# A fused attention and two-MLP kernel on one core: keys pooled by matmuls, a joined softmax, shared weight tiles and another order of stages

## The chip, the cores and the metric

The kernel runs on one core of a Trainium2 chip. The metric is the device time of one execution in microseconds (us); less is better. Three runs of the kernel before took 1649.82, 1650.77 and 1654.72 us; their median is 1650.77 us.

## The reference

Three layers follow one another (B = H = 8, S = 576, D = 64; 4608 tokens, model width 512, inner width 2048):

```python
k_p = k.reshape(B, H, 72, 8, D).mean(axis=3)      # keys and values pooled by 8
v_p = v.reshape(B, H, 72, 8, D).mean(axis=3)
scores = q @ k_p.T / sqrt(D)
attn = exp(scores - max(scores)); attn = attn / (sum(attn) + 1e-9)
x = (attn @ v_p) as tokens x 512                  # layer 0
h = x @ w_in_a                                    # layer 1: a rational function between two matmuls
x = ((a0 + a1 h + a2 h^2 + a3 h^3) / (1 + |b0||h| + |b1|h^2 + 1e-6)) @ w_out_a
out = relu(x @ w_in_b)^2 @ w_out_b                # layer 2
```

## The kernel before

**Tiling.** The tokens are cut into 36 chunks of 128 (for attention) and 9 blocks of 512 (for the two MLPs). Every fp32 matrix is split into a high and a low fp32r part, and a product is three matmul passes (high·high, high·low, low·high). One *slot* is one of 16 column groups of the inner width for one block: `mm1` (12 matmuls of 128x128 by 128x512), the function between (`first` and `second`, on VectorE and ScalarE), and three slots later (LAG = 3) `mm2` (12 matmuls). In the rational layer `first` and `second` put seven operations of 128x512 on VectorE and five on ScalarE; in layer 2 VectorE has one.

**Stages.** Blocks 0 and 1 come first, in 64 slots ("half"), while the weights are read and split (`w_raw`, `w_decode`) and written back to DRAM in split form. After that `w_fetch` reads a split weight tile (1 MB) for each slot. `SEQ` lists the stages after slot 63: `one` j is the rational layer of block j (16 slots), `two` 2 is layer 2 of block 2, and `pair` does layer 2 of two blocks at once by a seven-product scheme (28 slots of four steps with 6 matmuls each), with sums of the weights made beforehand (`w_sums`, `SUM_AT`) and seven combined inputs (`pair_forms`, tiles by `FORM_TAGS`). So the slots are: half 0 to 63, one 2 64 to 79, one 3 80 to 95, two 2 96 to 111, one 4 112 to 127, a gap of 3, pair (3,4) 131 to 158, one 5, one 6, gap, pair (5,6) 194 to 221, one 7, one 8, gap, pair (7,8).

**Attention.** `place_chunk` spreads each chunk over slots by `CHUNK_AT`: `q_split` at slot t, `qk`, `row_max` and `exps` at t + 2, `norm` at t + 4, `a_turn` or `a_split` at t + 5, `av` at t + 6, `x_out` at t + 7. The first nine chunks (c < NF) use fp32 matmuls on keys and values that are pooled on the core (`kv_first`): for the keys, `k_sum` reduces each of four 128x576 tiles on VectorE and scales it on ScalarE; for the values, `v_sum` pools by matmuls against a constant 0/1 matrix `sums`. The other 27 chunks use three-term bf16 products on keys and values that are pooled by adding DMAs of GpSimd's queue (`k_add`, `v_add`) and split by `k_split` and `v_split`. In `exps`, a half of a chunk in `WHOLE` takes one subtraction on VectorE, one exp on ScalarE and one sum on VectorE; any other half takes four exps on ScalarE, each with its own accumulated sum. `TURN_DVE` says which halves of the transposed weights VectorE copies out of PSUM; ScalarE copies the others. For blocks 0 to 2 (j < PLAIN) `x_out` writes the block's input straight into the tiles that `mm1` reads; for later blocks it writes to DRAM (`xd`), and `x_fetch` reads it back two slots ahead of the block.

**Order.** Nothing above is issued as it stands. `Plan` collects every operation with an assumed cost, runs a list scheduler with due times worked out backward, tries 96 variants and writes out one fixed order for each queue (TensorE, VectorE, ScalarE, GpSimd, SyncE). Each engine then works through its list in order. `run` adds lower limits: an attention operation placed at slot s (s at least 16, WINDOW = 8) isn't issued before the `mm1` (or pair step) of slot s - 8 has been; `w_sums` and `x_fetch` have no such limit. All instructions are recorded by one helper, so the profile gives nearly all of them the same line (L409), and they are told apart by their tiles: `h` and `y` are the PSUM banks of `mm1` and `mm2`, `x` and `w` inputs and weights, `sv`, `pq` and `g` the rational function, `xf`, `wi`, `gf`, `wo` the pair, `q`, `mx`, `e`, `sm`, `a`, `xo` a chunk, `kr` and `vr` the raw keys and values of the early chunks, `wv` and `ws` the weight sums.

Of the kernel before, what the change touches and what calls it, by code (L numbers as in the profile page):

```python
# [11 lines left out]
F32 = mybir.dt.float32  # L12
# [26 lines left out]
AHEAD, FIRST = 5.0, range(4)  # L39
FIRST_TWO = [0, 1]  # L40
PLAIN = 3
PAIRS = [(3, 4), (5, 6), (7, 8)]
SEQ = [
    ("one", 2), ("one", 3), ("two", 2), ("one", 4), ("pair", (3, 4)), ("one", 5), ("one", 6),
    ("pair", (5, 6)), ("one", 7), ("one", 8), ("pair", (7, 8)),
]
PAIR_SLOTS, PAIR_STEPS = 28, 4
NFT = DFF // 128
X_TAGS = {0: (4, 5), 1: (6, 0), 2: (1, 2), 3: (4, 5), 4: (6, 0), 5: (4, 5), 6: (6, 0), 7: (4, 5), 8: (6, 0)}
X_IN_W = {}  # L50
W_TAGS = {("one", j): (0, 1, 6, 7, 2, 3, 4, 5) for j in range(5, 9)}
W_TAGS |= {("one", 2): range(8), ("one", 3): range(8), ("one", 4): (0, 1, 3, 5, 6, 7, 2, 4)} | {("two", 2): (2, 3, 5, 6, 7)}
X2_TAGS = {3: "ya", 4: "yb", 5: "ya", 6: "yb", 7: "ya", 8: "yb"}
FORM_TAGS = {pair: dict(p1=1, p2=2, p5=3, p3=4, p6=5, p7=6, p4=0) for pair in PAIRS}
S_PLACES = ((0, 1, 2, 3), (2, 0, 3, 1))
LN_SHIFT = 60
SCALE = 1.0 / POOL / 8
# [2 lines left out]
QC = 1.0 + 1e-6  # L60
NF = 9
NORM_DVE = {0, 2, 3, 5} | set(range(8, NCHUNK))
WHOLE = {(c, 1) for c in range(NF)} | {(15, 1)}
TURN_DVE = {(c, 0) for c in range(NF)} | {(1, 1)}
BY_DMA = {(1, 1), (1, 3), (1, 5)}
KA, KB = 128 - SP, 2 * SP - 128
KC = SP + 2 * KB
# [3 lines left out]
NK = NF * CH // S  # L71
RAW_EARLY, STORE_EARLY, FETCH_EARLY, SUM_EARLY = 80.0, 25.0, 60.0, 40.0
SHIFT_ACT = {(1, f) for f in range(FH)} | {(3, 0), (3, 4)}
SUM_AT = {n: 49 + 4 * (n - 4) for n in range(4, 8)} | {n: 98 + 2 * n for n in range(4)}
CHUNK_AT = (
    {8 + n: 38 + 3 * n for n in range(8)} | {16 + n: 92 + 3 * n for n in range(6)}
    | {22 + n: 128 + 4 * n for n in range(6)} | {28 + n: 190 + 3 * n for n in range(8)}
)


# [335 lines left out]
def fused_kernel(  # L416
# [1 line left out]
    tc: tile.TileContext,  # L418
    qf: bass.AP,
    qt: bass.AP,  # L420
    kf: bass.AP,
    vn: bass.AP,
    vm: bass.AP,
    kt: bass.AP,
# [51 lines left out]
    def tt(n, out, in0, in1, op):  # L476
        dve(n, "tensor_tensor", out=out, in0=in0, in1=in1, op=op)
# [7 lines left out]
    def load(n, out, in_, early=None):  # L485
        plan.add("sp", 0.6, [(nc.sync.dma_start, dict(out=out, in_=in_))], n / LOAD_RATE, early)
# [19 lines left out]
    def h_bank():  # L506
        h_turn.append(0)
        return ps_h.tile([128, TB], F32, "h", f"h{len(h_turn) % 2}")
# [133 lines left out]
    def kv_first():  # L642


        k, v = ([p1.tile([128, 4 * TB], F32, n, f"x{o + i}") for i in range(2)] for o, n in ((0, "kr"), (2, "vr")))
        kr = [k[g // 3][:, g % 3 * S:(g % 3 + 1) * S].rearrange("p (k r) -> p k r", r=POOL) for g in range(H // 2)]
        vr = [v[c // 4][0:min(128, S - 128 * c), c % 4 * TB:(c % 4 + 1) * TB] for c in range(5)]
        for b, t in enumerate((k, v)):
            o = 1024 if b else S
            kp_t[b] = t[1][:, o:o + H // 2 * SP].rearrange("p (g k) -> p g k", g=H // 2)  # L650
            vp_t[b] = t[1][0:SP, 1536:2048]

        def k_sum(b):
            plan.ahead = K_AHEAD if b == 0 else 0.0
            for g in range(H // 2):
                load(128 * S * 4, kr[g], kf[b, g].rearrange("p (k r) -> p k r", r=POOL))
                dve(S, "tensor_reduce", out=kp_t[b][:, g], in_=kr[g], axis=AX.X, op=ALU.add)
                act(SP, AF.Copy, out=kp_t[b][:, g], in_=kp_t[b][:, g], scale=SCALE)
            if b == 0:
                q_first(0)  # L660

        def v_sum(b):
            plan.ahead = AHEAD if b == 0 else 0.0
            ps = h_bank()[0:SP]
            for c in range(5):
                n, o = min(128, S - 128 * c), S0W - 16 * c
                load(n * TB * 4, vr[c], vn[b, :, TB * c:TB * (c + 1)] if c < 4 else vm[b])
                pe(1.0, [dict(
                    out=ps, lhsT=sums[0:n, o:o + SP], rhs=vr[c], start=(c == 0), stop=(c == 4),
                )])  # L670
            act(DM, AF.Copy, out=vp_t[b], in_=ps)
            if b == 0:
                q_first(2)
                q_first(3)

        k_sum(0)
        plan.ahead = AHEAD
        q_first(1)
        v_sum(0)
        for c, fn in ((K1C, k_sum), (V1C, v_sum)):  # L680
            at(starts[c] + 5 if c >= 0 else -S0, "t", fn, 1)
# [120 lines left out]
    def exps(c, half):  # L802
        mx, sm, e = e_t[c]
        ps = sc_t.pop((c, half))
        hs = slice(half * (H // 2), (half + 1) * (H // 2))
        if (c, half) in WHOLE:
            n = H // 2 * SP
            tt(n, e[:, hs], ps, mx[:, hs].unsqueeze(2).to_broadcast([128, H // 2, SP]), ALU.subtract)
            act(n, AF.Exp, out=e[:, hs], in_=e[:, hs])
            dve(n, "tensor_reduce", out=sm[:, hs], in_=e[:, hs], axis=AX.X, op=ALU.add)  # L810
            return
        for hh in range(H // 2):
            h = half * (H // 2) + hh
            act(
                SP, AF.Exp, out=e[:, h, :], in_=ps[:, hh, :],
                bias=mx[:, h:h + 1], accum_out=sm[:, h:h + 1],
            )
# [83 lines left out]
    def x_out(c):  # L901
        ps = x_ps.pop(c)
        j, o = divmod(c, CPB)
        sc = 2.0 ** -A_SHIFT / POOL
        if j < PLAIN:
            if o == 0:
                xt[j] = [x_tile([128, 4, TB], "x", n) for n in X_TAGS[j]]
            x = [t[:, :, o * CH:(o + 1) * CH] for t in xt[j]]
        else:
            if o == 0:  # L910
                xd[j] = pd.tile([128, 2, 4, TB], F32, f"xd{j}")
            t = p2.tile([128, 2, 4, CH], F32R, "xo", "xs")
            x = [t[:, a] for a in (HI, LO)]
        act(TB, AF.Copy, out=x[HI], in_=ps, scale=sc)
        stt(TB, x[LO], ps, sc, f32(x[HI]), ALU.mult, ALU.subtract)
        if j >= PLAIN:
            for a in (HI, LO):
                load(2 ** 18, xd[j][:, a, :, o * CH:(o + 1) * CH], f32(x[a]))

# [40 lines left out]
    def evac(u):  # L960
# [16 lines left out]
        if ph == 1:  # L977
            for d in range(4):
                tt(TB, xt[j][LO][:, d], t[:, d], f32(xt[j][HI][:, d]), ALU.subtract)

    def evac_one(j):
        y = yps.pop(("one", j))
        if j < PLAIN:
            for d in range(4):
                act(TB, AF.Copy, out=xt[j][HI][:, d], in_=y[d])
                tt(TB, xt[j][LO][:, d], y[d], f32(xt[j][HI][:, d]), ALU.subtract)
            return
        if len(X2_TAGS[j]) == 2 and X2_TAGS[j][0] == "y":
            t = p1.tile([128, 4, TB], F32, "xm", X2_TAGS[j])
            x2[j] = [t[:, 0:2], t[:, 2:4]]  # L990
        else:
            x2[j] = [p2.tile([128, 2, TB], F32, "xm", X2_TAGS[j]) for _ in range(2)]
        for d in range(4):
            act(TB, AF.Copy, out=x2[j][d // 2][:, d % 2], in_=y[d])
# [239 lines left out]
    def run(slot, key):  # L1234
        for fn, args in todo.pop((slot, key), []):
            if args and args[0] in FIRST and fn in (k_add, v_add, q_load, qk, row_max, exps, norm, a_turn, av, x_out):
                plan.ahead = AHEAD
            if fn not in (w_raw, w_decode, w_sums, x_fetch, pair_forms) and slot >= GATED:
                plan.after = started.get(slot - WINDOW)
            if fn.__name__ in ("k_sum", "v_sum"):  # L1240
                plan.after = turned.get(K1C if fn.__name__ == "k_sum" else V1C)
            fn(*args)
            plan.ahead, plan.after = 0.0, None
# [44 lines left out]


    slots = [("half", (j, ph), f) for ph in range(4) for j in FIRST_TWO for f in range(FH)]  # L1290
    begins = {}
    for what, x in SEQ:
        if what == "pair" and slots[-1][0] == "one":
            slots += [("gap", None, None)] * LAG
        begins[what, x] = len(slots)
        slots += [(what, x, f) for f in range(PAIR_SLOTS if what == "pair" else NFT)]
    N = len(slots)
    steps = {pair: pair_steps(pair) for pair in PAIRS}
    for n, t in SUM_AT.items():
        for part in range(2):  # L1300
            at(t + 2 * part if n >= 4 else t, "x", w_sums, n, part, "w1" if n < 4 and part else "x3")
    for j in range(PLAIN, NB):
        at(begins["one", j] - 2, "x", x_fetch, j)
    FORMS_AT = {
        pair: begins["pair", pair] - 1 for pair in PAIRS
# [6 lines left out]
    def tile_slot(i):  # L1312

        what, x, f = slots[i]
        if what == "half":
            j, ph = x
            return j, ph // 2, wt_of[ph, f], x, f == 0, f == FH - 1, evac
        layer = int(what == "two")
        if i not in wf_t:
            wf_t[i] = w_fetch(x, layer, f)  # L1320
        done = evac_two if layer else evac_one
        return x, layer, wf_t[i], (what, x), f == 0, f == NFT - 1, lambda u: done(u[1])

# [79 lines left out]
```

## Time and profile before

| | |
|---|---|
| median of three runs | 1650.77 us |
| the profiled execution: time, span | 1649.59 us, 1647.9 us |
| TensorE, VectorE, ScalarE busy | 98 %, 86 %, 69 % |
| mean granted TensorE clock | 0.996 of full speed |
| moved by DMA | 401 MB, 244 GB/s over the span |

Busy shares are averages over stages with different limits. A matmul is issued before the one ahead of it has ended, so TensorE's busy time also covers short stalls; how many matmuls a stretch holds tells more.

### The profile page before, as it was taken

Reading aid. Unit: us, or ns where it says so; the run is one execution under the profiler, and the core shown is the slowest. Engines: PE = TensorE matmul, PEld = TensorE weight load, DVE = VectorE, ACT = ScalarE, POOL = GpSimd, SP = SyncE. Lnnn points to the kernel's source line nnn. Section 1 sums busy time; section 2 is a strip of 40 time slices with the busy share of each in tenths; the row PEclk is TensorE's granted clock in tenths of the full one; section 3 lists DMA queues with packets and bytes.
Section 4 is the critical chain, followed back from the end, with each engine's and each line's share of the span. In section 5 each row is a group of like instructions: output and inputs, shape, how many; then the busy total and the mean of one; then the engine's idle time right before and its main releaser. Section 6 shows DMA issues by size and latency. Waiting matters only on the chain.

```text
span 1647.9 us, 23637 instructions
## 1 busy us (share of the span) xinstructions
PE 1610.9 (98%) x8476; PEld 1307.3 (79%) x8476; DVE 1410.0 (86%) x2135; ACT 1132.6 (69%) x2105; POOL 77.8 (5%) x95
## 2 busy tenths in 40 slices
PE   7899999999999999999999999999999999999998
PEld 4678888888888877877787878887888788888886
DVE  7999998589889998488979788999889799996666
ACT  5989778787557766566787645667987466657553
POOL 0001100100001000001111000010000000000000
PEclk9999999999999999999999999999999999999999
DMA  7357578997999879999999996785799985555544
GB/s 269 131 231 196 152 265 298 241 257 250 313 299 286 289 258 274 322 270 279 258 243 281 283 321 245 233 244 190 227 267 263 292 291 200 185 185 171 191 154 141
DMA packets 199141, 401.43 MB, mean 244 GB/s; under 512 B 68752, under 2 KB 118768, under 8 KB 170864
## 3 DMA queue, kind: packets, MB, share of 16 engines
q1 hardware_dynamic: 188512, 379.76, 70.6%
q0 software_dynamic: 10512, 20.16, 7.8%
q8 instruction: 67, 1.10, 0.3%
q14 instruction: 50, 0.41, 0.1%
HBM read 310.91 MB, written 72.35 MB: 233 GB/s over the span
## 4 chain that ended last, share of the span: by engine, by line
PE 70%; DVE 19%; ACT 4%; DMA 3%; issue 2%; SPq 0%; ACTq 0%; DVEq 0%
PE h L409 30%; PE y L409 22%; DVE pq L409 7%; PE yx L409 7%; PE yz L409 5%; PE hz L409 5%; DVE g L409 3%; DVE sv L409 2%; ACT sv L409 2%; PE xp L409 1%; PE sc L409 1%; DMA xd<-xo 1%; DMA t<-a 1%; DVE t L409 1%; DVE wv L409 1%
## 5 line engine op out<-in xcount | busy, mean ns | idle before, releaser
L409 PE MATMUL h<-x,w 128*128 128x512 f32 x2304 | 557.8, 392 | 10.7 <-DVE pq L409 5.1
L409 PEld LDWEIGHTS h<-x,w 128*128 128x128 f32 x2304 | 430.8, 188 | 107.5 <-DVE pq L409 8.9
L409 PE MATMUL y<-g,w 128*128 128x512 f32 x1728 | 418.8, 391 | 3.7 <-DVE g L409 3.6
L409 PEld LDWEIGHTS y<-g,w 128*128 128x128 f32 x1728 | 324.1, 188 | 73.7 <-DVE g L409 6.3
L409 ACT ACTIVATE sv<-sv,cs 128x512 f32<-128x512 f32 x288 | 208.3, 724 | 154.7 <-DVE sv L409 149.8
L409 ACT ACTIVATE sv<-h 128x512 f32<-128x512 f32 x192 | 114.0, 594 | 68.1 <-PE h L409 52.7
L409 PE MATMUL h<-xf,wi 128*128 128x512 f32 x576 | 145.7, 391 | 0.7 <-ACT gb L409 0.5
L409 PE MATMUL yx<-gf,wo 128*128 128x512 f32 x576 | 142.8, 391 | 0.4 <-DVE acc L409 0.4
L409 PE MATMUL y<-w,g 128*128 128x512 f32 x576 | 140.4, 392 | 0.1
L409 ACT ACTIVATE pq<-h,cs 128x512 f32<-128x512 f32 x144 | 111.8, 776 | 24.4 <-PE h L409 14.0
L409 PEld LDWEIGHTS yx<-gf,wo 128*128 128x128 f32 x576 | 107.6, 188 | 24.3 <-issue 0.8
L409 PEld LDWEIGHTS h<-xf,wi 128*128 128x128 f32 x576 | 107.4, 188 | 23.8 <-ACT gb L409 1.4
L409 PEld LDWEIGHTS y<-w,g 128*128 128x128 f32 x576 | 107.2, 188 | 23.3 <-DVE g L409 0.5
L409 DVE SCALAR_TENSOR_TENSOR g<-pq,cs,sv 128x512 fp32r<-128x512 f32 x144 | 107.6, 747 | 19.5 <-ACT sv L409 16.9
L409 DVE SCALAR_TENSOR_TENSOR sv<-sv,cs 128x512 f32<-128x512 f32 x144 | 107.3, 745 | 14.4 <-ACT sv L409 14.3
L409 ACT ACTIVATE sv<-h,cs 128x512 f32<-128x512 f32 x144 | 98.8, 686 | 25.0 <-DVE g L409 15.9
L409 PE MATMUL hz<-xf,wi 128*128 128x512 f32 x432 | 110.2, 392 | 1.8 <-DVE ga L409 1.0
L409 PE MATMUL yz<-gf,wo 128*128 128x512 f32 x432 | 108.3, 392 | 3.1 <-DVE gf L409 1.5
L409 DVE SCALAR_TENSOR_TENSOR pq<-pq,cs 128x512 f32<-128x512 f32 x144 | 107.5, 747 | 1.9
L409 DVE SCALAR_TENSOR_TENSOR pq<-pq,cs,h 128x512 f32<-128x512 f32 x144 | 106.7, 741 | 0.6 <-ACT sv L409 0.2
L409 DVE TENSOR_TENSOR pq<-pq,h 128x512 f32<-128x512 f32 x144 | 98.0, 680 | 8.4 <-ACT pq L409 5.2
L409 DVE SCALAR_TENSOR_TENSOR pq<-sv,g 128x512 f32<-128x512 f32 x144 | 99.1, 688 | 2.8
(147 smaller groups left out, 2072.6 us busy)
## 6 DMA issues: line engine op xcount, KB each, us to landing
w<-ws SPq DMA_DIRECT2D x128, 1024.0 KB, 6.3
ws<-w SPq DMA_DIRECT2D x32, 1024.0 KB, 4.9
wi<-wf SPq DMA_DIRECT2D x48, 512.0 KB, 5.2
wo<-wf SPq DMA_DIRECT2D x48, 512.0 KB, 5.9
wo<-ws SPq DMA_DIRECT2D x72, 256.0 KB, 4.2
raw<-wa SPq DMA_DIRECT2D x16, 1024.0 KB, 6.7
raw<-wb SPq DMA_DIRECT2D x16, 1024.0 KB, 8.1
wf<-ws SPq DMA_DIRECT2D x16, 1024.0 KB, 9.2
```

Of the source, the lines that this page charges most:

```text
L409: made = fn(**{k: v.real() if isinstance(v, View) else v for k, v in kw.items()})
```

## The change

- `k_sum` pools the keys of the first two batches by matmuls: five loads of 128 (the last 64) rows of 512, four matmuls each against `sums`, one scaled copy out of PSUM. The host lays the keys out as it does the values.
- For the first nine chunks both halves are in `WHOLE`, and their exp and sum are joined into one operation each (`MERGED`); `TURN_DVE` is empty.
- The rational layers of the two blocks of a pair become one stage `both` (a, b) of 32 slots: the first 8 slots of a, all 16 of b, the last 8 of a. A weight tile is fetched once and used for both blocks (`kept`). The first half of a's output is copied out of PSUM (`evac_half`), and the second is added to it on VectorE.
- The pair's blocks are named in the other order, (4, 3) for (3, 4), and the tiles of the seven forms are given out anew.
- Layer 2 of block 2 moves from slots 96 to 111 to slots 112 to 127, behind the rational layers of blocks 3 and 4; its weight sums move along, with a lower limit.
- Block 3's input is written straight into its tiles (`DIRECT`).
- Chunks 8 to 15 stay. Chunks 16 to 19 move from slots 92 to 101 to slots 62, 66, 70 and 74; chunks 20 to 27 from 104 to 148 to 114 to 149, one each 5 slots; chunks 28 to 35 from 190 to 211 to 166 to 208, one each 6 slots.

```diff
-PAIRS = [(3, 4), (5, 6), (7, 8)]
+PAIRS = [(4, 3), (6, 5), (8, 7)]
 SEQ = [
-    ("one", 2), ("one", 3), ("two", 2), ("one", 4), ("pair", (3, 4)), ("one", 5), ("one", 6),
-    ("pair", (5, 6)), ("one", 7), ("one", 8), ("pair", (7, 8)),
+    ("one", 2), ("both", (3, 4)), ("two", 2), ("pair", (4, 3)), ("both", (5, 6)), ("pair", (6, 5)),
+    ("both", (7, 8)), ("pair", (8, 7)),
 ]
+DIRECT = {0, 1, 2, 3}
...
-FORM_TAGS = {pair: dict(p1=1, p2=2, p5=3, p3=4, p6=5, p7=6, p4=0) for pair in PAIRS}
+FORM_TAGS = {pair: dict(p1=1, p2=2, p5=3, p6=6, p3=0, p7=4, p4=5) for pair in PAIRS[1:]}
+FORM_TAGS[PAIRS[0]] = dict(p1=4, p2=5, p5=6, p6=0, p3=3, p7=1, p4=2)
...
-WHOLE = {(c, 1) for c in range(NF)} | {(15, 1)}
-TURN_DVE = {(c, 0) for c in range(NF)} | {(1, 1)}
+MERGED = set(range(NF))
+WHOLE = {(c, h) for c in MERGED for h in range(2)} | {(15, 1)}
+TURN_DVE = set()
...
-SUM_AT = {n: 49 + 4 * (n - 4) for n in range(4, 8)} | {n: 98 + 2 * n for n in range(4)}
+SUM_AT = {n: 49 + 4 * (n - 4) for n in range(4, 8)} | {n: 114 + 2 * n for n in range(4)}
 CHUNK_AT = (
-    {8 + n: 38 + 3 * n for n in range(8)} | {16 + n: 92 + 3 * n for n in range(6)}
-    | {22 + n: 128 + 4 * n for n in range(6)} | {28 + n: 190 + 3 * n for n in range(8)}
+    {8 + n: 38 + 3 * n for n in range(4)} | {12 + n: 50 + 3 * n for n in range(4)} | {16 + n: 62 + 4 * n for n in range(4)}
+    | {20 + n: 114 + 5 * n for n in range(8)} | {28 + n: 166 + 6 * n for n in range(8)}
 )
...
         def k_sum(b):
             plan.ahead = K_AHEAD if b == 0 else 0.0
-            for g in range(H // 2):
-                load(128 * S * 4, kr[g], kf[b, g].rearrange("p (k r) -> p k r", r=POOL))
-                dve(S, "tensor_reduce", out=kp_t[b][:, g], in_=kr[g], axis=AX.X, op=ALU.add)
-                act(SP, AF.Copy, out=kp_t[b][:, g], in_=kp_t[b][:, g], scale=SCALE)
+            ps = h_bank()[:, 0:H // 2 * SP].rearrange("p (g k) -> p g k", g=H // 2)
+            for c in range(5):
+                n = min(128, S - 128 * c)
+                load(n * TB * 4, kr[c], kn[b, :, TB * c:TB * (c + 1)] if c < 4 else km[b])
+                m = n // POOL
+                pe(0.4, [dict(
+                    out=ps[:, g, 16 * c:16 * c + m], lhsT=kr[c][:, 128 * g:128 * (g + 1)],
+                    rhs=sums[0:n, S0W:S0W + m], start=True, stop=True,
+                ) for g in range(H // 2)])
+            act(H // 2 * SP, AF.Copy, out=kp_t[b], in_=ps, scale=SCALE)
...
             tt(n, e[:, hs], ps, mx[:, hs].unsqueeze(2).to_broadcast([128, H // 2, SP]), ALU.subtract)
+            if c in MERGED:
+                if half == 0:
+                    return
+                n, hs = H * SP, slice(0, H)
             act(n, AF.Exp, out=e[:, hs], in_=e[:, hs])
             dve(n, "tensor_reduce", out=sm[:, hs], in_=e[:, hs], axis=AX.X, op=ALU.add)
...
+    def evac_half(j):
+        y = yps.pop(("half one", j))
+        t = p1.tile([128, 4, TB], F32, "xm", X2_TAGS[j])
+        ysb[j] = t
+        for d in range(4):
+            act(TB, AF.Copy, out=t[:, d], in_=y[d])
+
     def evac_one(j):
         y = yps.pop(("one", j))
+        if j in ysb:
+            t = ysb.pop(j)
+            for d in range(4):
+                tt(TB, t[:, d], y[d], t[:, d], ALU.add)
+            x2[j] = [t[:, 0:2], t[:, 2:4]]
+            return
...
+            if fn is w_sums and args[0] < 4:
+                plan.after = started.get(slot - 2)
...
+        if what == "both":
+            a, b = x
+            begins["one", a], begins["one", b] = len(slots), len(slots) + FH
+            for f in range(FH):
+                kept[len(slots) + FH + f] = len(slots) + f
+                kept[len(slots) + 3 * FH + f] = len(slots) + 2 * FH + f
+            slots += [("one", a, f) for f in range(FH)] + [("one", b, f) for f in range(NFT)]
+            slots += [("one", a, f) for f in range(FH, NFT)]
+            continue
```

## Rows read from the trace of the kernel before

**Rows 1.** The page, part 1: TensorE, busy us, share of the span, instructions

```profile
PE 1610.9 (98%) x8476; PEld 1307.3 (79%) x8476; DVE 1410.0 (86%) x2135; ACT 1132.6 (69%) x2105; POOL 77.8 (5%) x95
```

**Rows 2.** Whom TensorE waited for: us in total, times, longest

```profile
PE y L409 <- DMA q<-qf: 7.9, 1, 7.9
PE h L409 <- DVE pq L409: 5.1, 9, 1.4
PE y L409 <- DVE g L409: 3.6, 5, 1.6
...
PE h L409 <- DMA w<-ws: 1.9, 1, 1.9
```

**Rows 3.** The chain that ended last: start, us, what

```profile
104.97 2.72 PE y L409 x12
```

**Rows 4.** Stretches: length, busy (count) of PE, PEld, DVE, ACT, POOL; clock; DMA

```profile
20.00:40.00 20.00, 16.48 (x155) 10.29 (x154) 19.34 (x35) 13.95 (x36) 0.00 (x0) 0.83 0.66 210
40.00:60.00 20.00, 15.41 (x89) 11.77 (x87) 20.00 (x35) 19.25 (x44) 0.00 (x0) 1.00 0.58 209
...
280.00:362.00 82.00, 82.00 (x496) 67.11 (x495) 53.08 (x80) 64.86 (x136) 10.54 (x12) 1.00 0.92 242
362.00:420.00 58.00, 58.00 (x405) 47.68 (x404) 51.49 (x100) 38.11 (x87) 0.00 (x0) 1.00 0.86 257
420.00:530.00 110.00, 109.69 (x524) 90.22 (x523) 101.08 (x156) 68.27 (x106) 8.81 (x10) 1.00 0.91 299
...
530.00:600.00 70.00, 69.29 (x345) 56.70 (x344) 69.49 (x111) 50.46 (x87) 3.78 (x4) 1.00 0.84 271
640.00:700.00 60.00, 58.13 (x330) 47.35 (x330) 31.47 (x60) 33.28 (x87) 0.90 (x1) 0.97 0.99 303
700.00:760.00 60.00, 57.39 (x245) 45.04 (x244) 46.77 (x72) 36.10 (x58) 4.36 (x5) 1.00 0.96 289
940.00:980.00 40.00, 38.61 (x208) 30.66 (x207) 33.97 (x46) 18.84 (x27) 0.00 (x0) 1.00 0.97 314
1340.00:1380.00 40.00, 40.00 (x178) 33.14 (x177) 36.64 (x56) 25.30 (x40) 0.00 (x0) 1.00 0.56 190
```

**Rows 5.** Tiles q, mx, sm, a, xo, k, v: busy (count), VectorE next to last, ScalarE last

```profile
240.00:1300.00 1060.00, 0.00 (x0) 0.00 (x0) 66.03 (x54) 56.72 (x54) 1.00 0.89 268
...
240.00:1300.00 1060.00, 24.68 (x58) 73.32 (x432) 1.00 0.89 268
...
240.00:1300.00 1060.00, 32.21 (x86) 0.00 (x0) 1.00 0.89 268
...
240.00:1300.00 1060.00, 33.55 (x108) 18.41 (x27) 1.00 0.89 268
...
240.00:1300.00 1060.00, 15.78 (x24) 14.00 (x24) 1.00 0.89 268
...
240.00:1300.00 1060.00, 25.81 (x720) 10.72 (x18) 7.57 (x11) 1.00 0.89 268
...
240.00:1300.00 1060.00, 21.39 (x720) 19.22 (x720) 8.14 (x12) 7.48 (x12) 1.00 0.89 268
```

**Rows 6.** VectorE and ScalarE by shape: busy us, mean ns, idle before

```profile
L409 DVE COPY t<-t 64x1024 bf16<-64x1024 bf16 x27 | 11.2, 416 | 0.3
L409 DVE TENSOR_REDUCE vr<-kr 128x72 f32<-128x576 f32 x4 | 2.8, 730 | 0.0
L409 DVE TENSOR_TENSOR e<-xp,mx 128x288 f32<-128x288 f32 x6 | 2.7, 450 | 0.0
L409 DVE TENSOR_REDUCE sm<-e 128x4 f32<-128x288 f32 x10 | 4.4, 439 | 0.2 <-ACT e L409 0.2
L409 DVE COPY t<-sc 72x512 f32<-72x512 f32 x5 | 3.4, 679 | 0.3 <-PE sc L409 0.3
...
L409 ACT ACTIVATE e<-sc,mx 128x72 f32<-128x72 f32 x128 | 39.6, 320 | 7.6 <-DVE mx L409 7.6
```

**Rows 7.** TensorE in order of time: start, us, what

```profile
39.69 5.74 PE L409 MATMUL h<-x,w 128*128 128x512 f32 x24
```

More of the change, by code (lines that the diff above doesn't have):

```diff
@@ L51 @@
 W_TAGS = {("one", j): (0, 1, 6, 7, 2, 3, 4, 5) for j in range(5, 9)}
-W_TAGS |= {("one", 2): range(8), ("one", 3): range(8), ("one", 4): (0, 1, 3, 5, 6, 7, 2, 4)} | {("two", 2): (2, 3, 5, 6, 7)}
+W_TAGS |= {("one", j): range(8) for j in range(2, 5)} | {("two", 2): (2, 3, 5, 6, 7)}
 X2_TAGS = {3: "ya", 4: "yb", 5: "ya", 6: "yb", 7: "ya", 8: "yb"}
-FORM_TAGS = {pair: dict(p1=1, p2=2, p5=3, p3=4, p6=5, p7=6, p4=0) for pair in PAIRS}
+FORM_TAGS = {pair: dict(p1=1, p2=2, p5=3, p6=6, p3=0, p7=4, p4=5) for pair in PAIRS[1:]}
+FORM_TAGS[PAIRS[0]] = dict(p1=4, p2=5, p5=6, p6=0, p3=3, p7=1, p4=2)
 S_PLACES = ((0, 1, 2, 3), (2, 0, 3, 1))
@@ L420, in fused_kernel @@
     qt: bass.AP,
-    kf: bass.AP,
+    kn: bass.AP,
+    km: bass.AP,
     vn: bass.AP,
@@ L645, in kv_first @@
         k, v = ([p1.tile([128, 4 * TB], F32, n, f"x{o + i}") for i in range(2)] for o, n in ((0, "kr"), (2, "vr")))
-        kr = [k[g // 3][:, g % 3 * S:(g % 3 + 1) * S].rearrange("p (k r) -> p k r", r=POOL) for g in range(H // 2)]
-        vr = [v[c // 4][0:min(128, S - 128 * c), c % 4 * TB:(c % 4 + 1) * TB] for c in range(5)]
+        kr, vr = (
+            [t[c // 4][0:min(128, S - 128 * c), c % 4 * TB:(c % 4 + 1) * TB] for c in range(5)] for t in (k, v)
+        )
         for b, t in enumerate((k, v)):
-            o = 1024 if b else S
-            kp_t[b] = t[1][:, o:o + H // 2 * SP].rearrange("p (g k) -> p g k", g=H // 2)
+            kp_t[b] = t[1][:, 1024:1024 + H // 2 * SP].rearrange("p (g k) -> p g k", g=H // 2)
             vp_t[b] = t[1][0:SP, 1536:2048]
@@ L904, in x_out @@
         sc = 2.0 ** -A_SHIFT / POOL
-        if j < PLAIN:
+        if j in DIRECT:
             if o == 0:
@@ L915, in x_out @@
         stt(TB, x[LO], ps, sc, f32(x[HI]), ALU.mult, ALU.subtract)
-        if j >= PLAIN:
+        if j not in DIRECT:
             for a in (HI, LO):
@@ L1290, in fused_kernel @@
     slots = [("half", (j, ph), f) for ph in range(4) for j in FIRST_TWO for f in range(FH)]
-    begins = {}
+    begins, kept = {}, {}
+    halved = {x[0] for what, x in SEQ if what == "both"}
     for what, x in SEQ:
-        if what == "pair" and slots[-1][0] == "one":
+        if what == "pair":
             slots += [("gap", None, None)] * LAG
+        if what == "both":
[7 more added lines that the diff above has]
+            continue
         begins[what, x] = len(slots)
@@ L1301, in fused_kernel @@
             at(t + 2 * part if n >= 4 else t, "x", w_sums, n, part, "w1" if n < 4 and part else "x3")
-    for j in range(PLAIN, NB):
+    for j in set(range(NB)) - DIRECT:
         at(begins["one", j] - 2, "x", x_fetch, j)
@@ L1319, in tile_slot @@
         if i not in wf_t:
-            wf_t[i] = w_fetch(x, layer, f)
+            wf_t[i] = wf_t[kept[i]] if i in kept else w_fetch(x, layer, f)
+        if x in halved and not layer:
+            u, done = (what, x) if f >= FH else ("half one", x), evac_one if f >= FH else evac_half
+            return x, layer, wf_t[i], u, f % FH == 0, f % FH == FH - 1, lambda u: done(u[1])
         done = evac_two if layer else evac_one
@@ L1377 @@
     }
-    arrays["kf"] = lay(k[:NK].reshape(NK, H // 2, 2, S, D).transpose(0, 1, 2, 4, 3)).reshape(NK, H // 2, 2 * D, S)
-    a = v[:NK].transpose(0, 2, 1, 3).reshape(NK, S, DM)
-    arrays["vn"] = lay(
-        a[:, :S // 128 * 128].reshape(NK, S // 128, 128, DM).transpose(0, 2, 1, 3)
-    ).reshape(NK, 128, S // 128 * DM)
-    arrays["vm"] = lay(a[:, S // 128 * 128:])
+    for n, x in (("k", k), ("v", v)):
+        x = x[:NK].transpose(0, 2, 1, 3).reshape(NK, S, DM)
+        arrays[n + "n"] = lay(
+            x[:, :S // 128 * 128].reshape(NK, S // 128, 128, DM).transpose(0, 2, 1, 3)
+        ).reshape(NK, 128, S // 128 * DM)
+        arrays[n + "m"] = lay(x[:, S // 128 * 128:])
     for n, m in (("a", "moe_"), ("b", "moe2_")):
```

## The prediction

> **What bounds the kernel now.** I read the page's busy shares first: TensorE 98 %, VectorE 86 % [rows 1]. That share hides short stalls, so next came the chain of waits, where twelve matmuls of 128x512 in a full stream take 2.72 us [rows 3], 0.2267 us each. The program has 276 slots of 24 such matmuls: 6624 x 0.2267 = 1502 us of 1648. The chunks' small matmuls add about 27 x 1.75 = 47 us (from the k and v rows, 25.81 and 21.39 us of TensorE for 27 late chunks [rows 5]). So 99 us of the span are stalls and the early chunks' matmuls, and 39.7 of these lie before the first block matmul, which starts at 39.69 [rows 7]. The change leaves all 6624 matmuls; only stalls can move.
>
> The table of whom TensorE waited for names, behind the first loads (7.9 us), VectorE's rational operations (`pq` 5.1, `g` 3.6) and one weight load (1.9) [rows 2]. The table by stretch then says where [rows 4]. From 20 to 60 VectorE has no room (19.34 and 20.00 of 20): it is the bound, with ScalarE close behind (19.25 from 40 to 60). From 280 to 362 TensorE is always busy and VectorE has 29 us to spare. From 530 to 600 VectorE is full (69.49 of 70), yet TensorE idles only 0.71. From 640 to 760 both idle in turn: VectorE works 31.47 of 60 in layer 2 of block 2, then TensorE idles 2.61 of 60 while the rational pipeline of block 4 refills and stalls. From 940 to 980 TensorE idles 1.39 at the change from pair to one-block stage. In a late rational stage VectorE needs 36.64 us while TensorE does 178 matmuls in 40 [rows 4]: 4.94 us a slot against 5.44. The two engines are within 10 % of each other there, so any other VectorE work put into a rational stage costs TensorE time once 0.5 us a slot is used up.
>
> **The change part by part**, against the profiled execution (1649.59 us, span 1647.9).
>
> *Pooling by matmuls.* Eight reductions of 0.73 us leave VectorE [rows 6]. The first four wait for their loads, and what replaces them (four small matmuls behind the last load, one copy) ends at about the same time: 0, bounds -0.7 to +0.7. The second four lie in the full stretch between 20 and 40: 4 x 0.73 = 2.9 us earlier for the first block matmul. 20 pooling matmuls a batch are new on TensorE; no row shows an fp32 weight tile of 128 columns with 16 moving columns. From below they are free, as TensorE idles 3.5 us from 20 to 40 [rows 4]; from above each costs a whole 0.2267, 4.5 us, hidden or not. I take 0 since TensorE isn't the bound there.
>
> *Joined softmax.* For each of nine chunks VectorE gains a subtraction (0.45) and a longer sum (576 columns as in the key reduction, 0.73, for 0.44) and loses a copy (0.68) [rows 6]: +0.06 us, so +0.5 in all. ScalarE loses four exps of 0.32 with their accumulator reads, and gains a copy and half an exp: about 1 us less a chunk. ScalarE isn't ahead of VectorE in those stretches, so I take 0; if it were the bound of 40 to 60, up to 3 us would go. Head together: -2.9, bounds -6 to +2.
>
> *Chunks 16 to 19 moved to slots 62 to 74.* This is the term that decides. One late chunk costs VectorE, from the tile rows over 27 chunks (24 for `xo`, 29 for `mx`, of which each has two reductions, and 86/3 for `sm`): q 66.03/27 = 2.45, mx 0.85, sm 1.12, a 1.24, xo 0.66 [rows 5], and a copy of 0.42 [rows 6]: 6.74 us. Four are 27.0, and the split of a batch's keys and values is 10.72/6 + 8.14/6 = 3.1 [rows 5]: demand 30.1. The limit of eight slots lets chunk 16 begin at slot 54 and chunk 19 at slot 66; block 4 needs its input at slot 88. Slot 64 is near 420 us, so slot 54 is near 362 and slot 88 near 420 + 24 x 5.44 = 551; the last store to DRAM and the load back take the end of that, so the work must be done by about 530. VectorE's room there is 58 - 51.49 + 110 - 101.08 = 15.4 us [rows 4]; the four chunks' matmuls lengthen TensorE's own work by 4 x 1.75 = 7.0 us, which is room too. 30.1 - 15.4 - 7.0 = 7.7 us that TensorE must wait. The 29 us of room before 362 can't be used, as the limit forbids it. Bounds: +2 if the weight sums of the same stretch get out of the way, +18 if hardly any of chunks 16 to 19 is done before slot 64. Where they came from, 530 to 600 falls free: -0.7. Net +7.0.
>
> *Layer 2 of block 2 behind both.* The refill behind it disappears, since a pair follows: the 2.61 us idle of 700 to 760 go [rows 4], -2.6, bounds 0 to -3.3. In layer 2 itself TensorE idled 1.87 from 640 to 700 [rows 4], for a weight load that came late [rows 2]. That stage keeps its five weight tiles and its sums, but has four chunks beside it for about six: -1.4, bounds -2.5 to +2. The weight sums move with it; VectorE has 28 us to spare there, so 0.
>
> *Shared weight tiles, block 3 direct.* 48 weight loads of 1 MB and 4 MB of `xd` traffic leave the queues, from 401 MB in all. The rows of the late rational stage show TensorE without a gap at a DMA share of 0.56 [rows 4]: the loads were hidden, so 0; in 420 to 530 (share 0.91) it may help, in the bounds above. Each `both` has one more emptying of PSUM, on ScalarE, which is 63 % busy there (25.30 of 40): 0. Chunks 28 to 31 now lie in `both` (5, 6), as fillers without a near due time: +0.5, bounds 0 to 4.
>
> *Ends of pairs.* Block 5's chunks are done long before pair (4,3) ends, and the tiles of its input (x4, x5) hold the forms that go first: -1.2 of the 1.39 idle from 940 to 980 [rows 4]. For block 7 the same tiles hold forms p7 and p4, the fifth and last: its loads start one or two steps later, +0.5, bounds 0 to 3.
>
> Sum: -2.9 + 7.0 - 2.6 - 1.4 + 0.5 - 1.2 + 0.5 = -0.1, 1649.5 us. The median of the runs stands 1.2 above the profiled execution, so 1650.7; I say 1650.
>
> The Trainium skill has a rule on this order. Perfetto Trace Analysis, section Optimization Strategy, says that where the most contended engine changes over time, interleaving those regimes may help; here the new order puts three rational blocks in a row where layer 2 stood between the second and the third. The trace bears it out in part, in the 28 us of VectorE room from 640 to 700 that such an order leaves unused [rows 4]; by the rule the time would come out as in the second rival below.
>
> **The rivals.**
>
> *Faster, 1639.* The overload doesn't arise: the list scheduler fills the holes of 362 to 530 and shifts weight sums, so that it costs 2 and not 7.7, and the head gives 5 since ScalarE was also a bound (19.25 of 20 [rows 4]). 1649.6 - 5 + 2 - 0.7 - 2.6 - 1.9 - 1.4 = 1640.0; with the DMA relief in 420 to 530, 1639. For it: from 530 to 600 a full VectorE held TensorE up by only 0.71 [rows 4]. Against it: that stretch met its demand by spreading six chunks over longer.
>
> *Slower, 1661.* Three rational blocks in a row are a regime that VectorE bounds. Chunks 17 to 19 all fall behind slot 64, where 24 slots offer 24 x 0.5 = 12 us and block 2's own work takes part; their 23 us and the batch's split end late, block 4's input with them, and TensorE waits some 18 us before slot 88: 1649.5 + 18 - 7.7 + 1.2 = 1661. It decides once less than one of the four chunks is done before slot 64. For it: the holes of 362 to 420 are 6.5 us [rows 4], less than one chunk's 6.74. Against it: chunk 16 and part of 17 may start in that stretch.
>
> *The sharing is the point.* If weight loads held TensorE up in many short stalls, 48 fewer would show in every rational stage. One wait of 1.9 us in all [rows 2] speaks against it: no gain from it.
>
> **How the numbers follow.** Forecast (no change) 0.39, faster rival 0.37, slower rival 0.24, the third within the first. A measurement of this kernel tells apart about 0.3 %, 5 us: 1645 to 1656 counts as the same. The likeliest case alone has 1643 to 1657; the range takes in both rivals with some of their spread, 1635 to 1664, about 2 in 10 left out. Faster 0.38, the same 0.37, slower 0.25.
>
> **What would show it.** The first block matmul starts near 37 us. From slot 54 to slot 88 (about 360 to 555 us) VectorE is busy throughout and TensorE idles or loses some 8 us, with waits for `pq` and `g`; no such waits there proves the overload step wrong, waits of 15 us and more or a wait for `x` at block 4 prove the second rival. The gaps behind layer 2 of block 2 and at the end of the first pair are gone. A late rational stage runs as before at 178 matmuls in 40 us with less DMA; if it runs with gaps, the fillers in `both` cost more than 0.5. The prediction is wrong as a whole if the head moves by more than 6 us or a stage behind slot 131 by more than 5.

## The result and the profile after

The change makes the kernel slower: 1662.71 us (1659.46 to 1669.09, 7 runs) against 1651.48 (1648.96 to 1654.72, 7 runs), a ratio of 1.0063 [1.0047, 1.0079]. The prediction said 1650 and called "no change" the likeliest. The profiled execution has a span of 1661.0 us, 13.1 more than before.

Part 1 of the page after: busy us, share of the span, instructions of each engine.

```profile
PE 1626.7 (98%) x8556; PEld 1325.5 (80%) x8556; DVE 1409.9 (85%) x2138; ACT 1132.4 (68%) x2037; POOL 77.8 (5%) x95
```

VectorE does as much as before [rows 1]. TensorE has 15.8 us more of busy time and 80 more instructions. Its list in order of time says which (start, us, what, and in brackets the idle time ahead):

```profile
4.09 8.78 PE L412 MATMUL h<-sums,kr 128*128 128x16 f32 x40 [4.09 <-DMA kr<-kn]
13.37 3.69 PE L412 MATMUL y<-kr,q 64*128 64x72 f32 x32 [0.50 <-ACT kr L412]
...
30.17 1.06 PE L412 MATMUL h<-sums,kr 128*128 128x16 f32 x8 [1.19 <-DMA kr<-kn]
31.83 1.89 PE L412 MATMUL h<-sums,kr 128*128 128x16 f32 x8 [0.59 <-DMA kr<-kn]
...
37.27 5.24 PE L412 MATMUL h<-sums,kr 128*128 128x16 f32 x24
...
53.84 3.01 PE L412 MATMUL h<-x,w 128*128 128x512 f32 x12
```

The first block matmul starts at 53.84, not 39.69 [rows 7]: 14.15 later, which is more than the whole loss of the time (11.2 by the medians). The 20 pooling products of a batch appear as 40 instructions. Those of the first batch run without a gap for 8.78 us; the first scores follow at 13.37, where they began at 7.95 before. Those of the second batch take 1.06 + 1.89 + 5.24 = 8.19 us. Now the engines in the stretches that answer to the first of [rows 4]; columns as there.

```profile
20.00:40.00 20.00, 18.14 (x125) 14.11 (x123) 14.72 (x29) 13.21 (x26) 0.00 (x0) 0.79 0.79 266
40.00:54.00 14.00, 14.00 (x95) 8.30 (x95) 6.88 (x9) 6.49 (x9) 0.00 (x0) 0.69 0.44 153
```

Before, VectorE had no room here (19.34 and 20.00 of 20). Now it works 14.72 of 20 and 6.88 of 14, and TensorE is busy throughout from 40 to 54. What VectorE waited for between 4 and 54 (us in total, times, longest):

```profile
DVE mx L412 <- PE y L412: 17.7, 3, 14.0
DVE x L412 <- ACT x L412: 5.5, 1, 5.5
```

The bound of the head has changed engine: the row maxima wait for scores, which stand behind the pooling on TensorE.

Behind the head, here are the stretches that answer to the others of [rows 4], later by the shift of the same slots:

```profile
440.00:570.00 130.00, 126.56 (x738) 103.62 (x737) 128.23 (x218) 92.33 (x192) 5.93 (x7) 1.00 0.95 286
570.00:650.00 80.00, 80.00 (x354) 66.25 (x353) 72.11 (x109) 51.86 (x82) 7.03 (x8) 1.00 0.50 148
650.00:710.00 60.00, 60.00 (x266) 49.67 (x265) 55.12 (x81) 42.19 (x64) 5.17 (x6) 1.00 0.39 112
710.00:795.00 85.00, 83.79 (x451) 68.76 (x449) 70.82 (x121) 49.56 (x100) 0.90 (x1) 1.00 0.87 287
840.00:900.00 60.00, 56.42 (x279) 45.66 (x275) 44.61 (x65) 41.73 (x88) 5.96 (x7) 1.00 0.97 267
960.00:1000.00 40.00, 38.60 (x180) 30.18 (x179) 37.73 (x52) 20.12 (x30) 1.77 (x2) 1.00 0.96 325
1355.00:1395.00 40.00, 40.00 (x178) 33.10 (x178) 37.10 (x56) 26.74 (x44) 0.00 (x0) 1.00 0.17 59
```

The overload came where it was forecast (VectorE 128.23 of 130, TensorE idle 3.44), the rest of `both` runs without a gap (570 to 710), layer 2 of block 2 behind it (710 to 795) idles 1.21 where before it and the refill behind it idled 1.87 and 2.61 [rows 4], the gap at the end of the first pair is not (1.40 us), and a new one stands at the start of that pair (840 to 900, idle 3.58).

To compare stages in kernels whose work is ordered differently, I count a stage's loss: its length, less 0.2267 us for each block matmul and 0.0325 for each instruction of a late chunk's scores and `xp`. Slots are placed by counting block matmuls, so a figure is good to about 2 us.

| slots | before, SEED 0 / 1000 / 2000 | after | keys on VectorE, SEED 0 / 1000 / 2000 (e1, e11, e12) |
|---|---|---|---|
| 64 to 96 | 2.0 / -0.2 / -0.8 | 3.8 | 2.8 / 1.9 / 0.9 |
| 96 to 128 | 9.8 / 5.0 / 3.6 | 0.1 | -0.8 / -0.2 / -1.4 |
| 128 to 146 | 3.4 / 3.3 / 2.4 | 7.2 | 8.0 / 3.4 / 7.0 |
| 146 to 262 | 10.0 / 13.2 / 11.4 | 9.7 | 11.7 / 11.8 / 12.9 |

### The profile page after: what moved, and what is told of

Same layout as the page of the kernel before. It is cut to its first block, busy times and chain, and to the rows that moved or that the text cites. A ratio compares the mean times of both kernels' runs of the same rounds, so it can differ in the third digit from the quotient of the medians.

```text
span 1661.0 us, 23525 instructions
## 1 busy us (share of the span) xinstructions
PE 1626.7 (98%) x8556; PEld 1325.5 (80%) x8556; DVE 1409.9 (85%) x2138; ACT 1132.4 (68%) x2037; POOL 77.8 (5%) x95
## 4 chain that ended last, share of the span: by engine, by line
PE 69%; DVE 18%; DMA 6%; ACT 5%; issue 2%; SPq 0%; ACTq 0%; DVEq 0%
PE h L412 30%; PE y L412 22%; PE yx L412 6%; DVE pq L412 5%; PE yz L412 5%; PE hz L412 4%; DVE g L412 3%; DMA raw<-wb 1%; PE xp L412 1%; DVE sv L412 1%; DVE acc L412 1%; ACT sv L412 1%; DMA wf<-ws 1%; DVE raw L412 1%; PE sc L412 1%
## 5 line engine op out<-in xcount | busy, mean ns | idle before, releaser
L412 ACT ACTIVATE pq<-h,cs 128x512 f32<-128x512 f32 x144 | 112.6, 782 | 31.3 <-DVE g L412 17.7
L412 PEld LDWEIGHTS yz<-gf,wo 128*128 128x128 f32 x432 | 80.1, 188 | 26.6 <-DVE gf L412 2.8
```

The source lines that it names most:

```text
L412: made = fn(**{k: v.real() if isinstance(v, View) else v for k, v in kw.items()})
```

## The experiments

Theory A: the whole loss is TensorE's time for the fp32 pooling products, ahead of the first block matmul. Rivals: B, the crowded slots 54 to 88 (the slower rival of the prediction); C, the joined softmax. In each run the kernel before ran on the same chip.

**e1: the change with the keys on VectorE again.** `k_sum` and the host's layout of the keys are those of before.

```diff
-            ps = h_bank()[:, 0:H // 2 * SP].rearrange(...)
-            for c in range(5):
-                ...
-                pe(0.4, [dict(out=ps[:, g, ...], lhsT=kr[c][...], rhs=sums[...]) for g in ...])
+            for g in range(H // 2):
+                load(128 * S * 4, kr[g], kf[b, g].rearrange("p (k r) -> p k r", r=POOL))
+                dve(S, "tensor_reduce", out=kp_t[b][:, g], in_=kr[g], axis=AX.X, op=ALU.add)
+                act(SP, AF.Copy, ...)
```

> The changed kernel with one part undone: the keys of both early batches are reduced on VectorE again, everything else as changed. Theory A (the 40 pooling instructions of a batch hold TensorE for 8.8 us, 0.22 us each, and delay everything behind them): the first block matmul goes from 53.8 us back to 36 to 41, and the time falls by 12 to 16, to 1647 to 1651. Theory B (the joined softmax with its copies on ScalarE lengthens the early chunks' chain): the first block matmul stays beyond 46 and the time at 1657 or more. Theory C (three rational blocks in a row overload VectorE, the second rival of the prediction): the head improves, but the time stays near 1660.

Measured: 1651.72, ratio 1.0011 [0.9999, 1.0024]; first block matmul at 42.60. 11.0 us come back, so B and C are no cause of the loss. The first block matmul comes 2.9 later than in the kernel before, and a little later than expected.

**e2: the reverse, matmul pooling alone in the kernel before.** The diff is e1's, turned round.

> The kernel before with one part of the change alone: keys pooled by matmuls. Theory A: first block matmul at 50 to 54 us, time 1651.5 + 11 to 14 = 1662 to 1666. Theory B or C: no more than 3 us from 1651.5.

Measured: 1652.26, ratio 1.0009 [0.9996, 1.0023], though the first block matmul starts at 52.36. The expectation missed: the head lost 12.67 us and the time did not. The planner had made a new order of the whole kernel, and with it the stalls of slots 96 to 128 went from 9.8 to 1.1 us. e6, e7 and the other orders below take this apart.

**e3: joined softmax alone in the kernel before.**

```diff
-WHOLE = {(c, 1) for c in range(NF)} | {(15, 1)}
-TURN_DVE = {(c, 0) for c in range(NF)} | {(1, 1)}
+MERGED = set(range(NF))
+WHOLE = {(c, h) for c in MERGED for h in range(2)} | {(15, 1)}
+TURN_DVE = set()
```

> The kernel before with another part alone: joined softmax of the first nine chunks and all their transposed copies on ScalarE. Theory A: within 3 us of 1651.5, rather faster, since ScalarE does about 1 us less a chunk. Theory B: 1657 or more, with the first block matmul beyond 45 us.

Measured: 1651.04, ratio 0.9999 [0.9985, 1.0013]; first block matmul at 43.54, 3.85 later than before. C falls as a cause of the 11 us: the time is the same. What the joined softmax is worth within a few us can't be read from one order.

**e4: the planner is told a price near the traced one.** Its order is a list schedule by told costs; 0.4 us for four products becomes 1.75.

```diff
-                pe(0.4, [dict(
+                pe(1.75, [dict(
```

> The changed kernel, but the planner is told 1.75 us for each group of four pooling products instead of 0.4 (the trace shows eight instructions of 0.22 us). Nothing else differs; the order of issue is planned anew. If the loss is the pooling's own time on TensorE (theory A), it stays: 1657 to 1664. If most of it comes from an order planned with a price four times too low, it falls to 1652 or less.

Measured: 1664.78, ratio 1.0086 [1.0069, 1.0103], first block matmul at 55.75. The better price gave no better order; the time is even just above the expected range. That the products must be done before the scores, wherever they are put, is the likely reason.

**e5 and e6: cheap products in the identical order**, e5 in the change, e6 in e2's kernel. They read the upper 16 bits of each key as bf16, so the lower 16 bits of the first two batches' keys are left out.

```diff
-                    out=ps[...], lhsT=kr[c][:, 128 * g:128 * (g + 1)],
-                    rhs=sums[0:n, S0W:S0W + m], start=True, stop=True,
+                    out=ps[...], lhsT=kr[c][:, 128 * g:128 * (g + 1)].bitcast(BF16)
+                        .rearrange("p (n t) -> p n t", t=2)[:, :, 1],
+                    rhs=<the same view of sums>, start=True, stop=True,
```

> The changed kernel in exactly its own order of issue; only the pooling matmuls read the upper 16 bits of each fp32 key and of the 0/1 matrix as bf16 numbers (the lower 16 bits of the early keys are left out). Theory A (TensorE's time for the fp32 pooling is the loss): a batch takes 2 to 4 us instead of 8.8, the first block matmul comes at 40 to 45 us for 53.8, and the time falls by as much, to 1648 to 1654. Rival (the order planned around the pooling is the loss): 1658 or more.

> The kernel before with keys pooled by matmuls (as in the second experiment, in that one's order), the pooling again in bf16. There the first block matmul came 12 us late and the time stayed at 1652. If its order is simply better by 9 us later on (the stalls of slots 96 to 128 are gone) and a head delay counts in full, taking the delay away gives 1640 to 1645. If something later on absorbs any head delay, the time stays at 1650 to 1653.

Measured: e5 1651.06, ratio 0.9991 [0.9978, 1.0005]; e6 1641.88, ratio 0.993 [0.9913, 0.9947]. The products alone give back 11.65 and 10.38 us. TensorE in order of time in e5:

```profile
4.20 0.27 PE L412 MATMUL h<-sums,kr 128*128 128x16 bf16 x4 [4.20 <-DMA kr<-kn]
...
7.29 0.69 PE L412 MATMUL h<-sums,kr 128*128 128x16 bf16 x8 [1.01 <-DMA kr<-kn]
8.47 3.69 PE L412 MATMUL y<-kr,q 64*128 64x72 f32 x32 [0.50 <-ACT kr L412]
...
31.85 0.60 PE L412 MATMUL h<-sums,kr 128*128 128x16 bf16 x12
42.94 2.35 PE L412 MATMUL h<-x,w 128*128 128x512 f32 x9
```

One instruction a product now and gaps for the loads between them, so the loads bound the first scores again; the first block matmul is 10.90 earlier than after. A is shown, with its place: the same order without the fp32 products' time loses nothing against the kernel before. How much of that time the clock adds stands further down.

**e7: does a late head count in full?** The order of before is kept; 56 idle fp32 products stand ahead of the second batch's value pooling. They are work added to no end.

```diff
+            idle = [dict(out=ps[:, 0:CH], lhsT=sums[:, 0:SP], rhs=sums[:, 0:CH], start=True, stop=True)]
-                pe(1.0, [dict(
+                pe(1.0, (idle * 56 if b == 1 and c == 0 else []) + [dict(
```

> The kernel before in exactly its own order of issue, with 56 idle matmuls (fp32, 128 columns, about 0.21 us each) ahead of the second value pooling, so that TensorE reaches the first block matmul 10 to 13 us later. If a head delay counts in full: 1661 to 1664. If the layout of before absorbs it later: 1655 or less, with the lag against before shrinking somewhere behind slot 94.

Measured: 1661.19, ratio 1.0051 [1.0033, 1.0069].

```profile
26.18 13.42 PE L409 MATMUL h<-sums 128*72 128x128 f32 x112
49.03 5.73 PE L409 MATMUL h<-x,w 128*128 128x512 f32 x24
```

The first block matmul moves by 9.34 us and the time, against the kernel before measured beside it (1651.86), by 9.3. Nothing behind the head makes it up. So e2's even time was not slack behind a late head; e2's order saved elsewhere what its head lost.

**e8: the second batch alone back on VectorE.**

```diff
+            if b == 1:
+                <the loop of before>
+            else:
+                <the matmuls>
```

> The changed kernel with the keys of the second batch reduced on VectorE and those of the first still pooled by matmuls. The first batch delays the first scores from 7.95 to 13.4 us. If the two batches add up: first block matmul at 43 to 47 us and 1655 to 1659. If only the second matters, because the first chunks' softmax has slack: 1650 to 1653.

Measured: 1654.02, ratio 1.0008 [0.9996, 1.0021]; first block matmul at 44.50. The second batch gives back 8.7 of the 11.0 us; the time lies between the two ranges expected. The first scores still start at 13.96, yet the first block matmul is only 1.9 later than in e1: in this order most of the first batch's delay is made up within the head. The clock may help there, since e8 is granted 0.50 for 6.8 us of its head and e1 for 13.7.

**e9 to e18: the same kernels in other orders.** e6 beat the kernel before by 10 us. Is that the relief of VectorE, or an order that fell out well? The planner starts from a random number, and another one gives the same instructions in another order.

```diff
-SEED, TRIES = 0, 8
+SEED, TRIES = 1000, 8
```

> The kernel before with the planner's random start changed (SEED 1000 in place of 0): the same instructions in another order. Theory A (the pooling by fp32 matmuls costs the change 10 to 14 us, and the 10 us by which e6 beat the kernel before are the luck of a newly planned order): some new order of the same work moves the time by several us either way, so 1640 to 1660, with the losses of slots 96 to 128 changed the most. Rival (the 10 us come of the matmul pooling itself, which frees VectorE): another order of the same work gives 1648 to 1655, and the losses of slots 96 to 128 stay near 10 us.

> As e9_before_other_order_1 with SEED 2000. Theory A: 1640 to 1660, not the same as with SEED 1000. Rival: 1648 to 1655, with about 10 us lost in slots 96 to 128.

> The kernel of e1_keys_by_vector (the change without its matmul pooling) with SEED 1000. Theory A: the rest of the change is worth nothing by itself and the order some us either way, 1642 to 1660, first block matmul at 40 to 45 us. Rival (the rest of the change is worth its own loss at the second layers whatever the order): 1650 to 1654.

> As e11_vector_keys_other_order_1 with SEED 2000: theory A 1642 to 1660, rival 1650 to 1654.

> The kernel of e6 (before, keys pooled by matmuls that read the upper 16 bits of the keys as bf16, so their lower 16 bits are left out) with SEED 1000. Theory A (e6's 10 us are mostly the luck of its order): 1645 to 1655, spread like the orders of the kernel before (1648.0, 1651.6, 1654.7). Theory B (pooling by matmul takes eight reductions of 3.45 us from VectorE and is worth some 10 us once its products are cheap): 1639 to 1645 in every order.

> As e13_before_bf16_other_order_1 with SEED 2000. Theory A: 1645 to 1655; theory B: 1639 to 1645.

> The kernel of e5 (the change, with pooling products that read the upper 16 bits of the keys as bf16) with SEED 1000. Theory A: 1645 to 1655, spread like the change with keys on VectorE in three orders (1647.3, 1647.6, 1651.7). Theory B: 1638 to 1645, 8 to 10 us below the change with keys on VectorE in the same order, so that e5's 1651.1 was an unlucky order.

> As e15_after_bf16_other_order_1 with SEED 2000. Theory A: 1645 to 1655; theory B: 1638 to 1645.

> The change with SEED 1000. Theory A (the fp32 pooling products cost it 10 to 14 us at the first block matmul, whatever the order): first block matmul at 50 to 56 us, time 1656 to 1664, 8 to 14 us above the same with keys on VectorE in the order of SEED 1000 (e11: 1647.6). Rival (an unlucky order): 1645 to 1655.

> The change with SEED 2000. Theory A: first block matmul at 50 to 56 us, time 1656 to 1664, 8 to 14 us above e12 (1647.3). Rival: 1645 to 1655.

Measured, us, with the ratio to before (SEED 0) measured beside it:

| kernel | SEED 0 | SEED 1000 | SEED 2000 |
|---|---|---|---|
| before | 1651.57 | e9 1654.68, 1.0019 [1.0006, 1.0032] | e10 1648.02, 0.9975 [0.9966, 0.9984] |
| before, bf16 pooling | e6 1641.88 | e13 1645.85, 0.9976 [0.9965, 0.9987] | e14 1651.01, 1.0 [0.9987, 1.0013] |
| change, keys on VectorE | e1 1651.72 | e11 1647.62, 0.998 [0.9967, 0.9993] | e12 1647.34, 0.997 [0.9958, 0.9982] |
| change, bf16 pooling | e5 1651.06 | e15 1649.27, 0.9991 [0.9979, 1.0003] | e16 1650.98, 1.0 [0.9988, 1.0013] |
| change | 1662.71 | e17 1657.97, 1.0033 [1.0021, 1.0045] | e18 1661.84, 1.0057 [1.0038, 1.0075] |

An order alone moves the kernel before by up to 6.7 us, and e6's kernel by 9.1. No other order of that kernel, nor any of the change with bf16 products, comes down to 1645, so theory B of e13 falls, and e6's lead is at least in part its order. Of its 9.7 us 5.2 are left in the mean of three orders (1646.2 against 1651.4), while in the change the same pooling is 1.5 above the keys on VectorE (1650.4 against 1648.9); whether cheap pooling by matmul is worth a few us in the kernel before stays open with three orders each. The loss does not depend on the order: the change stands 11.0, 10.4 and 14.5 us above itself with keys on VectorE, and 11.7, 8.7 and 10.9 above itself with bf16 products. In e17 and e18 the first block matmul starts at 49.95 and 54.06, where e11 and e12 have 43.41 and 41.14; e17's head is 0.05 us short of the range expected and e18's distance from e12 0.5 beyond it. e18 repeats the picture of after:

```profile
4.06 8.79 PE L412 MATMUL h<-sums,kr 128*128 128x16 f32 x40 [4.06 <-DMA kr<-kn]
29.73 3.59 PE L412 MATMUL h<-sums,kr 128*128 128x16 f32 x16 [1.97 <-DMA kr<-kn]
36.87 5.24 PE L412 MATMUL h<-sums,kr 128*128 128x16 f32 x24
54.06 3.01 PE L412 MATMUL h<-x,w 128*128 128x512 f32 x12
```

e11 and e12, the change without its matmul pooling, leave nothing out and are faster than both kernels; but a new order of the kernel before (e10) gains about as much.

## Why the prediction was wrong

**Pooling by matmuls: the step that failed.** "I take 0 since TensorE isn't the bound there." In place of 0 the fp32 products cost 10.90 us of the head and 11.65 of the time (e5), and the 2.9 us that VectorE was to gain did not show (first block matmul at 42.94 in e5, at 42.60 in e1 with the keys on VectorE). It was wrong in three ways.

- The price. The bound from above was 20 whole block matmuls, 4.5 us a batch; the trace after has 8.78 and 8.19. Each fp32 product is two instructions, each with a weight load of 128 columns. The row of the first scores showed the two instructions before: 16 products, 32 instructions, 3.69 us. Forty at that rate are 4.6 us, on the path and not "hidden", and they took nearly twice that. A nearer row was that of the transposes, whose weight tiles have 128 rows like those of the products (64 in the scores): 16 instructions in 3.29 us, for the most part at a granted clock of 0.50, so forty are 8.2 us. Both are rows of TensorE in order of time, of the kernel before:

```profile
7.95 3.69 PE L409 MATMUL y<-kr,q 64*128 64x72 f32 x32 [7.95 <-DMA q<-qf]
...
29.76 3.29 PE L409 MATMUL y<-ident,e 128*72 128x128 f32 x16
```

- The place. "Hidden" was argued from idle time: 3.5 us in 20 to 40 [rows 4]. That was a share of a stretch, but TensorE takes its instructions in order: 24 pooling instructions of the second batch (37.27 to 42.5) stood ahead of the transposes and the value pooling of the next chunks, and everything behind those on ScalarE and VectorE waited, 5.5 us for `x` alone.
- The first batch. "Ends at about the same time" assumed loads as the bound. The products take 8.78 us from the first load on, and the scores start 5.42 later. With bf16 products, 0.52 later: only there do loads set it.

A rule on this stands in the Trainium skill, TensorE: Matmul & The Clock Gate, section Weight-path perf modes: the fast way to load weights is on when their number is 128 and the type is not fp32. The trace agrees in direction (at a granted clock of 0.50, 8 fp32 instructions take 1.89 us and 12 of bf16 0.60); how much of this is the load and how much the fp32 arithmetic, no run here separates.

**Where the 14.15 us of the head come from.** 10.90 go with the fp32 products (e5, same order). Part of them is the clock: after is granted 0.50 from 31.6 to 48.7 us, e5 only from 26.9 to 33.7, and the kernel before from 25.8 to 32.6. TensorE is busy for 15.97 of the 16.50 us from 31.3 to 47.8, and eight transposes take 1.92 us at 0.50 and 1.07 at 1.00, so the 10.2 us more at the lower level are an estimated 4.5 us of delay. The other orders of the change agree in direction: e17 has 10.2 us of its head at 0.50 and e18 20.5. No run held the level, so how the 10.90 divide is not shown. The other 3.25 stand in e1 (42.60) and e3 (43.54) too. Across orders of the kernel before the first block matmul lies between 38.88 and 43.06, so this may be the spread of an order. A price of the joined softmax is not excluded: with it and the keys on VectorE the head is at 0.50 for 13.7 us in all four runs (e1, e3, e11, e12), against 6.8, 6.8 and 10.2 in the orders of the kernel before. The forecast had -2.9 here, within -6 to +2; its own test, "wrong as a whole if the head moves by more than 6 us", decides.

**Joined softmax: 0.** The time agrees (e3), in the one order that was run.

**Chunks 16 to 19: +7.0.** The place and the sign were right, the size was not: slots 64 to 96 lose 0.9 to 3.8 us in the table's orders of the change against -0.8 to 2.0 before, some 1 to 3 us more. VectorE filled the stretch to 128.23 of 130. The count of room left out that the order can move other VectorE work to slots behind the crowd, where 570 to 650 has 8 us of room; that this made the difference is argued, not shown.

**Layer 2 of block 2: -4.0.** More than forecast: slots 96 to 128 lose nothing in any order of the change, against 9.8, 5.0 and 3.6. The refill went as forecast, and in layer 2 the idle time fell from 1.87 (in 60 us) to 1.21 (in 85). TensorE's waits from 605 to 800 before name `pq` (2.2 us), a weight load (1.9) and `g` (0.8), half of the 9.8; the other half no view names. In the second half of `both` the DMA share is 0.50 and 0.39, as the sharing removed loads; this was put at 0 and may have a part in it, which no run here separates.

**The start of the first pair: not foreseen.** Slots 128 to 146 lose 3.4 to 8.0 us against 2.4 to 3.4, more in three of the four orders. TensorE's waits from 780 to 960 after name it, a load of summed weights (`wf`) for the most part:

```profile
PE yz L412 <- DMA wo<-wf: 2.0, 1, 2.0
PE h L412 <- ACT gf L412: 1.1, 1, 1.1
```

In e1 it is the other weight, as its waits from 790 to 1000 show:

```profile
PE h L412 <- DMA wi<-wf: 2.7, 2, 2.1
```

The kernel before has no wait of TensorE for a load there. The weight sums moved with layer 2, from slots 98 to 104 to slots 114 to 120, and the pair still starts behind slot 128; the prediction asked whether VectorE has room for the sums (it has), not how soon they are read. But that their new time is the cause is not shown: after, the last store of sums is issued at 789.21, the loads of `wo` ahead of the wait, which ends at 851.76, only at 833.67 and 844.06, with the DMA engines 0.97 busy from 840 to 900. Why the loads come late stays open.

**Ends of pairs: -1.2.** Wrong: TensorE idles 1.40 from 960 to 1000, as it did 1.39 before [rows 4].

**Fillers in `both` (5, 6): +0.5.** Within its bounds: slots 146 to 262 lose 11.7 to 12.9 with keys on VectorE, 10.0 to 13.2 before. The late rational stage runs as before, 178 matmuls in 40 us at a DMA share of 0.17.

So without its pooling the change is worth about -2.5 us (1648.9 against 1651.4, means over three orders that spread as much); "no change" was right for that part, by terms that missed in both directions. The slower rival's 1661 came close to the time by accident. Its mechanism needed 18 us before slot 88, and e1, with the same crowded slots, loses none of the 11. By the Trainium skill's rule on interleaving regimes (Perfetto Trace Analysis, section Optimization Strategy), on which that rival leaned, the loss would have stood in those slots; the trace puts 1 to 3 us there.

## What to carry to other kernels

Work moved to an engine that is idle on average is priced by its instructions (an fp32 product is two, each with its own weight load) and by what stands behind them in that engine's queue, not by the idle share of the stretch; look for the nearest row of the same operand type and shape, not the best-known row. In this prologue, which no block matmul overlaps, a late head counted in full (e7). What is added where the granted clock has fallen costs more: an instruction of the pooling took 0.22 us there and 0.13 elsewhere. And where a planner orders the work anew on every edit, compare with the order kept, or over several orders: here an order alone was worth up to 9 us, nearly the size of the effect.

## What the runs showed of the hardware

The same fp32 pooling instruction took about 0.13 us at a granted clock of 1.00 and 0.22 at 0.50 (columns as in [rows 4], both of after):

```profile
30.00:31.30 1.30, 1.06 (x8) 0.97 (x8) 1.30 (x5) 1.30 (x2) 0.00 (x0) 1.00 0.85 279
37.20:42.50 5.30, 5.30 (x27) 5.24 (x25) 3.69 (x5) 1.66 (x3) 0.00 (x0) 0.50 0.90 273
```

The level of 0.50 (1.2 GHz, against 2.4) stood in the middle of the head, after TensorE had waited 1.19 and 0.59 us for loads of keys. In e7 the idle products start at 26.18 and the level is back at 1.00 from 28.2 on; in the kernel before, where TensorE waits 2.49 us ahead of 27.99, it is back at 32.6. The first batch's forty also took 0.22 each, though the view says 1.00 for their stretch:

```profile
4.00:13.00 9.00, 8.78 (x40) 8.68 (x40) 0.00 (x0) 0.09 (x1) 0.00 (x0) 1.00 0.86 282
```

That 1.00 is no measurement. The trace of after holds no record of the clock ahead of 21.4 us and that of the kernel before none ahead of 15.5, and a view counts 1.00 where there is none; the mean of 0.996 in the table of the kernel before does so too. The rates tell the level. The value pooling of the kernel before takes 0.79 us an instruction up to 16.3 us and 0.51 just behind:

```profile
11.57 4.73 PE L409 MATMUL h<-vr,sums 128*72 128x512 f32 x6
...
16.57 1.02 PE L409 MATMUL h<-vr,sums 128*72 128x512 f32 x2
```

So by their rate, an inference, the first batch's products ran at the lower level too.
